# Entries 0 and 1 of the feed-forward block: first product beside the remaining attention, second product by one level of Strassen's scheme

## The chip, the cores and the metric

The kernel runs as one program on one core of a Trainium2 chip. The metric is the device time of an execution in microseconds (us). Before the change it is 1051.8 us, the median of 3 runs (1049.94 to 1052.03).

The core has four engines that compute: TensorE (PE in the rows; its weight loads are PEld), VectorE (DVE), ScalarE (ACT) and GpSimd (POOL). SyncE (SP) issues all transfers here, from one queue in program order. Each engine works through its own list of instructions in order and waits at semaphores. The 16 DMA engines carry the transfers between HBM and on-chip memory.

## The reference

```
attn: (4 entries, 12 heads, 448 rows, 64)
  scores = cap * tanh(q k^T / sqrt(64) / cap);  attn = softmax(scores) v
x = attn, heads side by side              (4, 448, 768)
FFN: xn = layernorm(x) * g
     x  = x + relu(xn w1) w2              w1 (768, 3072), w2 (3072, 768)
gMLP: h = relu(x w_in), w_in (768, 1024); u, v = halves of h
     v = layernorm(v);  v = w_spatial v + b  (over the 448 rows)
     out = (u * v) w_out                  w_out (512, 768)
```

All is float32. Products that need it are made of three TensorE products in a reduced 32-bit format (fp32r): high by high, high by low, low by high part. The inputs that are weights reach the chip as 64-bit floats; ScalarE and VectorE turn each block into float32, and the result is kept in HBM for later use.

## The kernel before

The four entries are worked on in two pairs. **Attention of entries 0 and 1** comes first by itself. Then comes the **FFN of entries 0 and 1, with the attention of entries 2 and 3 beside it**: attention work of the 24 remaining heads is threaded between the matmul units. Then follow the gMLP of entries 0 and 1, the FFN of entries 2 and 3 with nothing beside it, and their gMLP.

The two FFNs are built differently. For entries 0 and 1 the 24 blocks of 128 hidden features are taken in 6 groups of 4: `h_units` makes 4 hidden blocks for both entries (18 matmuls of 448 columns each), which stay on chip in the slots `rb` as high and low part, and `y_units` at once multiplies them into all 6 output blocks (12 matmuls each) and adds the result to the residual in `x`. That is 864 matmuls for the first product and 864 for the second. For entries 2 and 3 both products go by one level of Strassen's scheme, 7 block products in place of 8: `h_four` makes the hidden blocks and writes them, and four mixtures of them, to HBM (`hidden`, 84 tiles of 448 columns), and `y_seven` reads them back product by product. A block product of `y_seven` is 6 steps (`g`) of 18 matmuls, so the second product is 7 x 6 x 18 = 756 matmuls. Its left sides are quarters of `w2` (`a11` to `a22`), or sums and differences of them made by VectorE; a quarter is read out of the kept `w2` in runs of 128 numbers (512 bytes).

The order of instructions on each engine is fixed ahead by a planner (`Program.plan`): it simulates the engines with a cost for each operation and picks, per engine, the ready operation that is due first, provided its buffers have room. Due times follow from the order of TensorE's work. An operation recorded under `prog.either()` may go to one of two engines: the second is taken where the first would keep it waiting longer. Operations under `prog.early()` get a due time of their own. Buffers are slots that go round; some of them belong to a `Stage`, memory that is handed to another set of buffers only when every buffer of the stage before it is free.

The names that matter here: `rs` (16 slots) right-hand sides in two parts, `wh` (3) weights in two parts, `wr` (2) weights as float32, `hs` (10) single tiles of 448 columns, `es` (7) exponentials, `qk` (2) queries and keys, `w` raw 64-bit weights, `kept_...` weights in HBM, `bank` (4) and `two` (2 of two banks) PSUM. In the rows nearly every instruction has line 532, that of the helper that records it, so rows are told apart by names and shapes.

## Time and profile before

| | |
|---|---|
| median of 3 runs | 1051.8 us |
| the profiled execution, whole | 1050.03 us |
| its span, first to last instruction | 1047.9 us |
| TensorE busy in the span | 1030.5 us |
| VectorE, ScalarE busy | 811.2, 501.4 us |
| moved by DMA | 180.25 MB |

The span is 2.1 us shorter than the execution. The stages of the span, by what TensorE does: attention of entries 0 and 1 to about 126.5 us; FFN of entries 0 and 1 with the other attention to 524.1; gMLP to about 633; `h_four` to 786.5; `y_seven` to 941.2; gMLP to the end. Busy times are of one execution; matmuls are pipelined, so that each is shown longer than the time from one to the next, and a busy TensorE is not by itself one at its peak. DMA share is the mean busy share of the 16 DMA engines; it can exceed 1, since packets overlap on an engine.

### The profile page before, as it was taken

Reading aid. Unit: us, or ns where it says so; the run is one execution under the profiler, and the core shown is the slowest. Engines: PE = TensorE matmul, PEld = TensorE weight load, DVE = VectorE, ACT = ScalarE, POOL = GpSimd, SP = SyncE. Lnnn points to the kernel's source line nnn. Section 1 sums busy time; section 2 is a strip of 40 time slices with the busy share of each in tenths; the row PEclk is TensorE's granted clock in tenths of the full one; section 3 lists DMA queues with packets and bytes.
Section 4 is the critical chain, followed back from the end, with each engine's and each line's share of the span. In section 5 each row is a group of like instructions: output and inputs, shape, how many; then the busy total and the mean of one; then the engine's idle time right before and its main releaser. Section 6 shows DMA issues by size and latency. Waiting matters only on the chain.

```text
span 1047.9 us, 14400 instructions
## 1 busy us (share of the span) xinstructions
PE 1030.5 (98%) x5182; PEld 849.7 (81%) x5182; DVE 811.2 (77%) x1395; ACT 501.4 (48%) x780; POOL 14.4 (1%) x19
## 2 busy tenths in 40 slices
PE   7999999999999999999999999999999999999998
PEld 2333698988898879888888889999999899998887
DVE  6979878585686775855979889887787897888971
ACT  7998744355426434453434345544462453324522
POOL 0000000000000000000000110000000000000000
PEclk9999999999999999999999999999999999999999
DMA  7444266467667565554455133455799968302303
GB/s 252 150 132 113 69 192 192 150 205 242 213 214 234 195 225 167 178 183 139 139 175 201 49 111 114 157 183 187 242 335 334 323 183 249 107 29 77 94 31 116
DMA packets 111212, 180.25 MB, mean 172 GB/s; under 512 B 18035, under 2 KB 82213, under 8 KB 111141
## 3 DMA queue, kind: packets, MB, share of 16 engines
q1 hardware_dynamic: 111140, 179.33, 53.9%
q8 instruction: 41, 0.67, 0.3%
q14 instruction: 31, 0.25, 0.1%
HBM read 127.99 MB, written 51.30 MB: 171 GB/s over the span
## 4 chain that ended last, share of the span: by engine, by line
PE 75%; DMA 10%; DVE 10%; ACT 2%; issue 2%; SPq 1%; POOL 0%; ACTq 0%; DVEq 0%; POOLq 0%
PE bank L532 58%; PE two L532 17%; DMA hs<-inv 2%; DVE x L532 2%; DMA inv<-rc 1%; DVE wr L532 1%; DMA qk<-in_qk_dram 1%; DVE wh L532 1%; DMA kept_w<-wr 1%; DMA w<-in_w_dram 1%; DVE es L532 1%; DVE rs L532 1%; DVE small L532 1%; SPq L532 1%; DVE rb L532 1%
## 5 line engine op out<-in xcount | busy, mean ns | idle before, releaser
L532 PE MATMUL bank<-rs,wh 128*128 128x448 f32 x1626 | 342.3, 363 | 3.3 <-DVE rs L532 1.3
L532 PEld LDWEIGHTS bank<-rs,wh 128*128 128x128 f32 x1626 | 304.1, 188 | 28.0 <-DVE wh L532 2.2
L532 PE MATMUL bank<-rb,wh 128*128 128x448 f32 x864 | 175.2, 363 | 0.0
L532 PEld LDWEIGHTS bank<-rb,wh 128*128 128x128 f32 x864 | 161.5, 187 | 12.4 <-DVE es L532 0.6
L532 ACT ACTIVATE wr<-w 128x512 f32<-128x512 f32 (+1 forms) x72 | 53.9, 749 | 112.3 <-DMA w<-in_w_dram 43.9
L532 DVE TENSOR_TENSOR wh<-wr,wh 128x512 fp32r<-128x512 f32 (+2 forms) x116 | 92.6, 801 | 8.9 <-ACT wh L532 6.9
L532 ACT ACTIVATE wh<-wr 128x768 fp32r<-128x768 f32 (+1 forms) x68 | 49.8, 733 | 59.7 <-PE bank L532 43.0
L532 DVE TENSOR_TENSOR x<-bank,x 128x448 f32<-128x448 f32 x95 | 58.7, 621 | 24.2 <-PE bank L532 23.3
L532 ACT ACTIVATE es<-es,capt 128x896 f32<-128x896 f32 x72 | 73.2, 1054 | 0.0
L532 ACT ACTIVATE es<-two,qsc 128x896 f32<-128x896 f32 x62 | 61.7, 1020 | 15.2 <-PE two L532 14.2
L532 PE MATMUL two<-rs,wh 128*128 128x448 f32 x276 | 64.6, 363 | 0.0
L532 DVE SCALAR_TENSOR_TENSOR wr<-w,wr 128x512 int32<-128x512 int32 (+1 forms) x80 | 63.2, 794 | 1.1
L532 PE MATMUL bank<-es,vt 128*64 128x448 f32 x288 | 62.2, 552 | 0.3 <-ACT hs L532 0.3
L532 DVE TENSOR_SCALAR wr<-wr 128x512 int32<-128x512 int32 (+1 forms) x76 | 35.6, 471 | 32.8 <-ACT wr L532 32.6
L532 ACT ACTIVATE hs<-bank 128x448 f32<-128x448 f32 x58 | 31.3, 541 | 53.4 <-PE bank L532 51.1
L532 PEld LDWEIGHTS two<-rs,wh 128*128 128x128 f32 x276 | 51.8, 188 | 3.9 <-DVE wh L532 0.3
L532 ACT ACTIVATE rb<-bank 128x448 fp32r<-128x448 f32 x48 | 26.0, 542 | 58.3 <-PE bank L532 58.0
L532 DVE SCALAR_TENSOR_TENSOR rb<-bank,rb 128x448 fp32r<-128x448 f32 x48 | 29.8, 621 | 30.9 <-ACT rb L532 30.8
L532 DVE TENSOR_TENSOR es<-es,es 128x896 f32<-128x896 f32 x48 | 52.0, 1084 | 0.4 <-ACT es L532 0.2
L532 ACT ACTIVATE rs<-hs 128x448 fp32r<-128x448 f32 x55 | 30.9, 572 | 36.1 <-DMA hs<-h 35.8
L532 DVE TENSOR_TENSOR rs<-hs,rs 128x448 fp32r<-128x448 f32 x75 | 45.5, 620 | 2.4 <-ACT rs L532 2.1
L532 PEld LDWEIGHTS bank<-es,vt 128*64 128x64 f32 x288 | 17.4, 136 | 36.5 <-issue 29.1
(185 smaller groups left out, 1515.6 us busy)
## 6 DMA issues: line engine op xcount, KB each, us to landing
hs<-h SPq DMA_DIRECT2D x84, 224.0 KB
w<-in_w_dram SPq DMA_DIRECT2D x24, 768.0 KB
w<-in_w_dram SPq DMA_DIRECT2D x36, 512.0 KB
qk<-in_qk_dram SPq DMA_DIRECT2D x24, 448.0 KB
h<-hs SPq DMA_DIRECT2D x48, 224.0 KB
kept_w<-wr SPq DMA_DIRECT2D x24, 384.0 KB
kept_w<-wr SPq DMA_DIRECT2D x36, 256.0 KB
wrb<-kept_w SPq DMA_DIRECT2D x24, 384.0 KB
```

The lines of the kernel that those rows point to most:

```text
L532: fn(*(put(a) for a in args), **{k: put(a) for k, a in kw.items()})
```

## The change

The FFN of entries 0 and 1 is cut into two phases. In the first, all 24 hidden blocks of both entries are made (`h_units`, now without groups), with all of the remaining attention beside them, spread over 93% of the phase. The hidden blocks go as single tiles into new slots (`hx`, 10); whenever two blocks of both entries are there, `mixed_h` makes four mixtures and writes all 7 to HBM. The 36 blocks of `w2` are turned into float32 and written to HBM in this phase too. In the second phase `y_seven`, until now used for entries 2 and 3 only, makes the second product. Beside its products 4, 5 and 3 the 16 blocks of `w_in` and `w_out` are turned into float32; before, those of the second half of `w_in` were made inside the gMLP, and the other 10 beside the FFN.

`y_seven` itself changes: the products come in the order 1, 2, 7, 6, 4, 5, 3 (before 1, 7, 6, 4, 5, 2, 3), other sums of blocks are formed, and in the first pass the 24 mixed weight blocks are written to HBM (`kept_s`) and read from there in the second. The stages are new as well: after `one` (attention and first phase) comes `mid` (weights of the second phase), then `gate` (buffers of the gMLP: `rbg`, `vsg`, `qkg`, `bsg`). The planner takes VectorE as second engine of an operation only where the wait for the first is more than 0.8 us longer than the operation itself.

Where the instructions went on TensorE, after the first hidden blocks (`rs` times `wh` into a `bank`, six rows to a block; `rb` are hidden blocks). Before:

```order
L532 MATMUL bank_138<-rs_76,wh_95 128x448 x3
L532 MATMUL bank_138<-rs_77,wh_95 128x448 x3
L532 MATMUL bank_138<-rs_78,wh_95 128x448 x3
L532 MATMUL bank_135<-rb_324,wh_96 128x448 x3
L532 MATMUL bank_135<-rb_325,wh_96 128x448 x3
L532 MATMUL bank_135<-rb_327,wh_96 128x448 x3
L532 MATMUL bank_135<-rb_328,wh_96 128x448 x3
```

And of the changed kernel, at the end of its 24 hidden blocks:

```order
L533 MATMUL bank_137<-rs_76,wh_95 128x448 x3
L533 MATMUL bank_137<-rs_77,wh_95 128x448 x3
L533 MATMUL bank_137<-rs_78,wh_95 128x448 x3
L533 MATMUL bank_140<-rs_63,wh_94 128x448 x3
L533 MATMUL bank_140<-rs_64,wh_94 128x448 x3
L533 MATMUL bank_139<-rs_63,wh_94 128x448 x3
L533 MATMUL bank_139<-rs_64,wh_94 128x448 x3
L533 MATMUL bank_138<-rs_63,wh_94 128x448 x3
L533 MATMUL bank_138<-rs_64,wh_94 128x448 x3
```

The second product followed a group of four hidden blocks out of `rb`; now it starts after the last hidden block, out of `rs`, into three banks at a time.

The transfer queue (SP) in the middle of the first phase, where `h` are hidden tiles and their mixtures on the way to HBM. Before, around the sums of the 6th of 12 pairs of heads of the remaining attention:

```order
L532 DMA kept_w_18_197<-wr_93 128x512
L532 DMA w_331<-in_w_dram 128x1024
L532 DMA kept_w_18_197<-wr_92 128x512
L532 DMA w_330<-in_w_dram 128x1536
L532 DMA vt_0_342<-in_v_dram 128x2x192
L532 DMA qk_339<-in_qk_dram 128x896
L532 DMA qk_340<-in_qk_dram 128x896
L532 DMA sum_10_191<-hs_82 4x448
L532 DMA x_6_186<-hs_84 128x448
```

And of the changed kernel:

```order
L533 DMA kept_w_18_223<-wc_458 128x512
L533 DMA w_460<-in_w_dram 128x1024
L533 DMA h_1_5_224<-hx_456 128x448
L533 DMA hs_83<-inv_6_199 64x448 x2
L533 DMA hs_81<-inv_6_199 64x448 x2
L533 DMA vt_0_463<-in_v_dram 128x2x192
L533 DMA h_2_4_214<-hx_451 128x448
L533 DMA h_6_4_216<-hx_448 128x448
L533 DMA qk_446<-in_qk_dram 128x896
L533 DMA qk_447<-in_qk_dram 128x896
L533 DMA h_7_5_229<-hx_455 128x448
L533 DMA sum_10_221<-hs_80 4x448
```

The writes of hidden tiles stand between the loads of weights and of the attention's inputs.

The transfer queue in `y_seven`: `hs` are hidden tiles read back, `wq` and `wqm` quarters of `w2`. Before (entries 2 and 3, product 6):

```order
L532 DMA wq_6145<-kept_w_18_197 128x6x128
L532 DMA hs_87<-h_6_281 128x448
L532 DMA hs_88<-h_7_288 128x448
L532 DMA wq_6146<-kept_w_24_209 128x6x128
L532 DMA hs_82<-h_8_295 128x448
L532 DMA wq_6147<-kept_w_30_218 128x6x128
L532 DMA hs_81<-h_9_302 128x448
```

And of the changed kernel in the second phase (entries 0 and 1, product 6):

```order
L533 DMA hs_82<-h_6_7_251 128x448
L533 DMA hs_83<-h_6_8_262 128x448
L533 DMA hs_81<-h_6_9_274 128x448
L533 DMA kept_s_0_308<-wqm_3239 128x768
L533 DMA kept_s_0_307<-wqm_3238 128x768
L533 DMA w6m_3250<-in_w_v_dram 128x1024
L533 DMA kept_s_1_310<-wqm_3241 128x768
L533 DMA kept_s_1_309<-wqm_3240 128x768
L533 DMA kept_s_2_312<-wqm_3243 128x768
L533 DMA w6m_3251<-in_w_v_dram 128x1024
L533 DMA hs_85<-h_6_10_285 128x448
```

The same reads of hidden tiles now share the queue with writes of mixed weights and reads of raw `w_in`.

The diff, cut to its core:

```diff
-FIRST = 8, 2, 7, 2
+FIRST = 2, 7, 2, 10, 2, 2
...
-AFTER = 0.3, 0.75, 6
+AFTER = 0.05, 0.9, 0.93
+LATER = 4, 5, 3
...
-                    if alt[k][1] > wait + BIAS:
+                    if alt[k][1] > wait + (BIAS if e != 'V' else -0.8):
...
+    tops = Stage(prog, tc, "sums", (), "right")
     one = Stage(prog, tc, "one")
-    two_h = Stage(prog, tc, "two_h", (one,), "right")
-    two_x = Stage(prog, tc, "two_x", (one,))
...
+    wqm, w6m, wcm = staged(mid, "wq", 18, "wqm"), staged(mid, "w6", 2, "w6m"), staged(mid, "wq", 2, "wcm")
+    rbg, vsg, qkg, bsg = (staged(gate, k, n, k + "g") for k, n in (("rb", 8), ("vt", 7), ("qk", 2), ("acc", 1)))
...
-    wq = staged(four, "wq", 4 * NG)
+    wq = staged(four, "wq", 18)
+    for stage in four, mid:
+        staged(stage, "gap", 1)
+    whf, whm = staged(four, "wh", 3, "whf"), staged(mid, "wh", 1, "whm")
...
-            value(kind, j)
+            value(kind, j, pool=raw6[1])
...
-            raw = w6.get()[:, 0:n]
+            raw = raw6[0 if n > DH else 2].get()[:, 0:n]
-            t = wr.get()[:, 0:n]
+            t = pool.get()[:, 0:n]
...
     def h_unit(b, w):
         hi, lo = w
         ps = banks.get()[:, 0:S]
         mm3(ps, [(hi[:, k], lo[:, k], x[:, 0], x[:, 1]) for k, x in enumerate(xn[b])])
-        t = rb1.get()
-        A.activation(out=t[:, 0, 0:S], in_=ps, func=ACTF.Relu)
-        V.scalar_tensor_tensor(out=t[:, 1, 0:S], in0=ps, scalar=0.0, in1=f(t[:, 0, 0:S]),
-                               op0=ALU.max, op1=ALU.subtract)
-        hq[b % 2].append(t)
-
+        h = hx.get()
+        relu(h, ps)
+        return h
+
+    def relu(o, c):
+        with prog.either():
+            A.activation(out=o, in_=c, func=ACTF.Relu)
+            V.tensor_scalar(out=o, in0=c, scalar1=0.0, scalar2=None, op0=ALU.max)
+
+    def mixed_h(i, h11, h12, h21, h22, t1, t2, t3, t4):
+
+        sub(t1, h12, h11)
+        sub(t2, h22, t1)
+        sub(t3, h22, h12)
+        sub(t4, h21, t2)
+        for n, t in ((1, h11), (3, h22), (2, h21), (5, t1), (6, t2), (7, t3), (4, t4)):
+            hidden[n, i] = dram.tile([128, S], F32, name=f"h{int(last_pass[0])}_{n}_{i}")
+            SP.dma_start(out=hidden[n, i], in_=t)
 
     ysp = []
-
-    def y_unit(b, w, dt, last):
...
-    def y_unit(b, w, dt, last):
-        hi, lo = w
-        ps = banks.get()[:, 0:S]
-        mm3(ps, [(hi[:, i], lo[:, i], h[:, 0, 0:S], h[:, 1, 0:S]) for i, h in enumerate(hq[b % 2])])
-        x = xts[b % 2][dt]
-        V.tensor_tensor(x, ps, x, ALU.add)
-        if last:
-            V.tensor_tensor(x, x, rst[b % 2], ALU.mult)
-            if b % 2 == 0:
-                ysp.append((rs.get(), rs.get()))
-            split_y(b, dt)
...
-            if n == 1:
-                return load(a11, g, wr)
+            if n in (1, 2) or n == 4 and last_pass[0]:
+                held[n, g] = load({1: a11, 2: a12, 4: a22}[n], g, wr if n == 1 else wq)
+                return held[n, g]
+            if last_pass[0]:
+                t = wq.get()[:, 0:HD * FW // 2]
+                SP.dma_start(out=t, in_=kept_s[n, g])
+                return t
             if n == 7:
-                held["a11", g], held["a21", g] = load(a11, g), load(a21, g)
-                t = wr.get()[:, 0:HD * FW // 2]
-                sub(t, held["a11", g], held["a21", g])
+                held["a21", g], t = load(a21, g), load(a11, g)
+                sub(t, t, held["a21", g])
+                keep_s(n, g, t)
+                held["s3", g] = t
                 return t
             if n == 6:
                 held["a22", g] = load(a22, g)
-                s1, s2 = held["a21", g], held["a11", g]
-                add(s1, s1, held["a22", g])
-                sub(s2, s1, s2)
+                s1, s2, x = held["a21", g], held["s3", g], held["a22", g]
+                add(s1, s1, x)
+                sub(s2, x, s2)
+                keep_s(5, g, s1)
+                keep_s(6, g, s2)
                 return s2
+            if n == 5:
+                return held["a21", g]
             if n == 4:
                 return held["a22", g]
-            if n == 5:
-                return held["a21", g]
-            if n == 2:
-                held["a12", g] = load(a12, g)
-                return held["a12", g]
-            s4 = held["a12", g]
-            sub(s4, s4, held["a11", g])
+            s4 = load(a12, g)
+            sub(s4, s4, held["s3", g])
+            keep_s(n, g, s4)
             return s4
+
+        def keep_s(n, g, t):
+            kept_s[n, g] = dram.tile([128, HD * FW // 2], F32, name=f"kept_s{n}_{g}")
+            with prog.early():
+                SP.dma_start(out=kept_s[n, g], in_=t)
 
         X = [banks.get()[:, 0:S] for _ in range(HD)]
         two = twos.get()
         Y = [two[:, 0, 0:S], two[:, 1, 0:S], banks.get()[:, 0:S]]
-        for n, o, start, stop in ((1, X, 1, 0), (7, Y, 1, 0), (6, X, 0, 0), (4, Y, 0, 1), (5, X, 0, 0), (2, None, 1, 1),
-                                  (3, X, 0, 1)):
-            if o is None:
+        beside = deque(beside)
+        two = twos.get()
+        W = [two[:, 0, 0:S], two[:, 1, 0:S]]
+        for n, o, start, stop in ((1, X, 1, 0), (2, W, 1, 1), (7, Y, 1, 0), (6, X, 0, 0), (4, Y, 0, 1), (5, X, 0, 1),
+                                  (3, W, 1, 1)):
+            if n == 2:
+                o = W + [Y[2]]
+            if n == 3:
                 two = twos.get()
                 o = [two[:, 0, 0:S], two[:, 1, 0:S], banks.get()[:, 0:S]]
             for g in range(NG):
+                if beside and n in LATER:
+                    ahead(*beside.popleft())
...
-                w = wh.get()[:, :, 0:HD * FW // 2]
+                w = (wh if n == 1 or g % 2 or g % 4 and not last_pass[0] else whf if last_pass[0] else whm).get()[:, :, 0:HD * FW // 2]
...
-                    t = (r2 if n != 1 and (g + k) % 3 == 0 else rs).get()
+                    t = (r2 if last_pass[0] and n != 1 and (g + k) % 3 == 0 else rs).get()
...
-            b, at, last = {1: (0, 0, 0), 7: (1, HD, 0), 6: (0, HD, 0), 4: (0, HD, 1), 5: (1, HD, 1), 2: (0, 0, 1),
-                           3: (1, 0, 1)}[n]
-            for d in range(HD):
-                y = xts[b][at + d]
-                add(y, o[d], y)
-            if last:
+            for b, at in {1: [(0, 0)], 2: [(0, 0)], 7: [(1, HD)], 6: [(0, HD)], 4: [(0, HD)], 5: [(1, HD), (1, 0)],
+                          3: [(1, 0)]}[n]:
+                for d in range(HD):
+                    y = xts[b][at + d]
+                    add(y, o[d], y)
+            for b, at in {2: [(0, 0)], 4: [(0, HD)], 5: [(1, HD)], 3: [(1, 0)]}.get(n, ()):
                 for d in range(HD):
...
+                    if not last_pass[0]:
+                        V.tensor_tensor(x, x, rst[b], ALU.mult)
...
-    def h_units(bs, g, n):
-
-        steps = [n, FG - n] if n > 2 else [2] * (FG // 2)
-        j0 = g * FG
-        for m in steps:
+    def h_units(bs):
+
+        j0 = 0
+        for m in (4, *[2] * (NF // 2 - 2)):
             w = [weight("w1", j0 + j) for j in range(m)]
-            j0 += m
+            mine = {}
             for b in bs:
                 for j in range(m):
-                    h_unit(b, w[j])
+                    mine[b, j] = h_unit(b, w[j])
                     if b in ln and j == 0:
                         ln_scale(b)
+                    if b % 2 and j % 2:
+                        h = [mine[e, i] for i in (j - 1, j) for e in bs]
+                        mixed_h((j0 + j) // 2, *h, *(hx.get() for _ in range(4)))
                     yield 3 * KD
-
-    def y_units(bs, g, last):
-        if last:
-            for b in bs:
-                xn.pop(b)
-        for dt in range(KD):
-            w = weight("w2", g * KD + dt)
-            for b in bs:
-                y_unit(b, w, dt, last)
-                yield 3 * FG
+            j0 += m
         for b in bs:
-            hq[b % 2].clear()
+            xn.pop(b)
...
-            units = chain(*(x for g in range(NG) for x in (
-                h_units(bs, g, FG if g == 0 and p == 0 else 3 if g == 0 else 2), y_units(bs, g, g == NG - 1))))
-            n = 2 * H if p + 1 < NP else 0
-            total = NG * 2 * (FG * 3 * KD + KD * 3 * FG)
-            todo = []
-            if p == 0:
-                later = [("wv", k) for k in range(KD)] + [("wu", i) for i in range(KH)] + [("wo", k) for k in range(KD)]
-                later = later[AFTER[2]:]
-                for j, x in enumerate(later):
-                    todo.append((total * (AFTER[0] + (AFTER[1] - AFTER[0]) * j / len(later)), ahead, x))
-            drive(units, todo + attend(2 * H * (p + 1), n, 2 * NG * (FG * 3 * KD + KD * 3 * FG) / max(n, 1)))
-            gmlp(bs, [b for b in (2 * p + 2, 2 * p + 3) if n])
+            total = NF * 2 * 3 * KD
+            rows = [("w2", j) for j in range(NG * KD)]
+            later = [("wv", k) for k in range(KD)] + [("wu", i) for i in range(KH)] + [("wo", k) for k in range(KD)]
+            todo = [(total * (AFTER[0] + (AFTER[1] - AFTER[0]) * j / len(rows)), ahead, x) for j, x in enumerate(rows)]
+            n = 2 * H
+            drive(h_units(bs), todo + attend(n, n, AFTER[2] * total / n))
+            raw6[:] = w6m, wcm, w6m
+            y_seven(wqm, later)
+            gmlp(bs, [2 * p + 2, 2 * p + 3])
 
     main()
+    tops.begin()
     one.begin()
     with tc.manual_schedule():
         t = tok_t[0][0]
```

## Rows read from the trace of the kernel before

**Rows 1.** The page: busy time by engine; granted TensorE clock in 40 slices.

```profile
PE 1030.5 (98%) x5182; PEld 849.7 (81%) x5182; DVE 811.2 (77%) x1395; ACT 501.4 (48%) x780; POOL 14.4 (1%) x19
...
PEclk9999999999999999999999999999999999999999
```

**Rows 2.** The page: the chain that ended last, share of the span.

```profile
PE 75%; DMA 10%; DVE 10%; ACT 2%; issue 2%; SPq 1%; POOL 0%; ACTq 0%; DVEq 0%; POOLq 0%
```

**Rows 3.** Busy times by stretch: FFN of entries 0, 1; last `y_seven`.

```profile
core 0: us, PE busy (x) PEld busy (x) DVE busy (x) ACT busy (x) POOL busy (x), PEclk, DMA share, GB/s
126.50:524.10 397.60, 396.45 (x2101) 337.87 (x2099) 283.78 (x464) 177.11 (x261) 1.01 (x1) 1.00 0.59 189
...
786.50:941.20 154.70, 153.73 (x758) 141.48 (x757) 129.16 (x206) 57.54 (x95) 0.00 (x0) 1.00 0.68 206
```

**Rows 4.** Groups of instructions: name and shape, count, busy us, mean ns.

```profile
L532 PE MATMUL bank<-rb,wh 128*128 128x448 f32 x864 | 175.2, 363 | 0.0
```

**Rows 5.** TensorE in order of time at 504 to 530 us: start, length, count.

```profile
503.69 17.17 PE L532 MATMUL bank<-rb,wh 128*128 128x448 f32 x85
520.79 2.48 PE L532 MATMUL bank<-es,vt 128*64 128x448 f32 x12
...
524.08 3.07 PE L532 MATMUL two<-wh,rs 128*128 128x512 f32 x12
...
529.09 1.10 PE L532 MATMUL two<-wh,rs 128*128 128x512 f32 x4
```

**Rows 6.** DMA issues: names, count, KB (1024 bytes) each.

```profile
hs<-h SPq DMA_DIRECT2D x84, 224.0 KB
...
wq<-kept_w SPq DMA_DIRECT2D x24, 384.0 KB
...
w<-in_w_u_dram SPq DMA_DIRECT2D x4, 768.0 KB
w<-in_w_out_dram SPq DMA_DIRECT2D x6, 512.0 KB
w<-in_w_v_dram SPq DMA_DIRECT2D x6, 512.0 KB
...
kept_wu<-wr SPq DMA_DIRECT2D x4, 384.0 KB
kept_wo<-wr SPq DMA_DIRECT2D x6, 256.0 KB
```

**Rows 7.** The same columns as rows 3, where the transfers were busiest.

```profile
785.00:835.00 50.00, 49.62 (x245) 45.24 (x243) 40.31 (x61) 18.72 (x31) 0.00 (x0) 1.00 1.10 337
760.00:780.00 20.00, 20.00 (x102) 18.75 (x101) 17.72 (x30) 14.24 (x26) 0.00 (x0) 1.00 1.02 352
550.00:560.00 10.00, 10.00 (x46) 8.34 (x45) 8.62 (x16) 6.39 (x12) 0.00 (x0) 1.00 1.03 380
```

**Rows 8.** Groups on VectorE, shapes apart.

```profile
L532 DVE SCALAR_TENSOR_TENSOR wr<-w,wr 128x512 int32<-128x512 int32 x48 | 32.8, 687 | 0.7
L532 DVE SCALAR_TENSOR_TENSOR wr<-w,wr 128x768 int32<-128x768 int32 x32 | 30.4, 953 | 0.4
...
L532 DVE TENSOR_SCALAR wr<-wr 128x512 int32<-128x512 int32 x48 | 20.2, 423 | 14.1 <-ACT wr L532 13.9
...
L532 DVE TENSOR_TENSOR wq<-wq,wq 128x768 f32<-128x768 f32 x18 | 17.1, 952 | 0.0
L532 DVE TENSOR_SCALAR wr<-wr 128x768 int32<-128x768 int32 x28 | 15.4, 554 | 18.8 <-ACT wr L532 18.7
...
L532 DVE TENSOR_TENSOR x<-x,rstd 128x448 f32<-128x448 f32 x24 | 14.3, 619 | 0.0
```

**Rows 9.** The same columns as rows 3: gMLP of entries 0, 1.

```profile
560.00:580.00 20.00, 20.00 (x101) 18.75 (x101) 19.76 (x49) 9.80 (x21) 2.34 (x2) 1.00 0.22 77
...
524.10:640.00 115.90, 114.14 (x549) 99.10 (x546) 101.27 (x199) 48.67 (x91) 9.03 (x6) 1.00 0.41 134
```

More of the change, by code (lines that the diff above doesn't have):

```diff
@@ L595, in staged @@
         return stage.slots(name or kind, n, shape, dt, protos[kind])
+    tops = Stage(prog, tc, "sums", (), "right")
     one = Stage(prog, tc, "one")
-    two_h = Stage(prog, tc, "two_h", (one,), "right")
-    two_x = Stage(prog, tc, "two_x", (one,))
+    mid = Stage(prog, tc, "mid", (one,))
+    gate = Stage(prog, tc, "gate", (mid,))
+    two_h = Stage(prog, tc, "two_h", (gate, tops), "right")
+    two_x = Stage(prog, tc, "two_x", (gate,))
     three_h = Stage(prog, tc, "three_h", (two_h,), "right")
@@ L602, in attn_ffn_gmlp_kernel @@
     three = Stage(prog, tc, "three", (four,))
-    rb1, w6, es1, qks = (staged(one, kind, n) for kind, n in zip(("rb", "w6", "es", "qk"), FIRST))
+    w6, es, qks, hx, wc, w4 = (
+        staged(one, kind, n, name) for (kind, name), n in zip(
+            (("w6", "w6"), ("es", "es"), ("qk", "qk"), ("acc", "hx"), ("wq", "wc"), ("w4", "w4")), FIRST))
     vts = [staged(one, "vt", 1, f"vt{i}_") for i in range(2)]
-    accs = [staged(one, "acc", 1, f"acc{i}_") for i in range(2)]
+    wqm, w6m, wcm = staged(mid, "wq", 18, "wqm"), staged(mid, "w6", 2, "w6m"), staged(mid, "wq", 2, "wcm")
+    rbg, vsg, qkg, bsg = (staged(gate, k, n, k + "g") for k, n in (("rb", 8), ("vt", 7), ("qk", 2), ("acc", 1)))
+    accs = [staged(tops, "acc", 1, f"acc{i}_") for i in range(2)]
     h2 = staged(two_h, "acc", 6, "hh")
@@ L963, in ln_load, with feature_sum @@
             SP.dma_start(out=xts[b % 2][k], in_=xsp[b, k])
-    def feature_sum(ps, x, pool=rb1):
+    def feature_sum(ps, x, pool=wh):
         t = pool.get()[:, :, 0:S]
@@ L977, in ln_mean @@
         ps = banks.get()[:, 0:S]
-        feature_sum(ps, accof[b])
+        feature_sum(ps, accof[b], rs if b >= 2 else wh)
         means[b] = rst[b % 2] if b >= 2 else hs.get()
@@ L1063, in v_mm @@
         os = [t[:, j] for t in two for j in range(2)] + [banks.get() for _ in range(len(cs) - 4)]
-        single = (0, 1, KD // 2, KD // 2 + 1, KD // 2 + 2, KD - 1) if last_pass[0] else (0, KD - 1)
-        order = [*range(KD // 2, KD), *range(KD // 2)] if last_pass[0] else [*range(KD)]
+        single = 0, 1, KD // 2, KD // 2 + 1, KD // 2 + 2, KD - 1
+        order = [*range(KD // 2, KD), *range(KD // 2)]
         for at, k in enumerate(order):
@@ L1078, in v_mm @@
                     part.close()
-        if last_pass[0]:
-            vs = [vs3.get() for _ in os]
-        else:
-            vs = [es.get().rearrange("p a n -> p (a n)")[:, 0:DH] for _ in os]
+        vs = [(vs3 if last_pass[0] else vsg).get() for _ in os]
         for vi, o in zip(vs, os):
@@ L1140, in sp_units @@
                                  stop=(b % 2 == 1 and c == half - 1 and m == 2))
-        xs = None if last_pass[0] else qks.get()
+        xs = None if last_pass[0] else qkg.get()
         for b, ps in zip(bs, pss):
@@ L1193, in gmlp @@
             scale(b)
-        bias = xts[0][KD - 1] if last_pass[0] else vts[0].get()[:, 0:S]
+        bias = xts[0][KD - 1] if last_pass[0] else bsg.get()
         SP.dma_start(out=bias, in_=b_sp)
@@ L1404, in snap @@
             A.activation(out=o, in_=ps, func=ACTF.Copy)
-        def relu(o, c):
-            with prog.either():
-                A.activation(out=o, in_=c, func=ACTF.Relu)
-                V.tensor_scalar(out=o, in0=c, scalar1=0.0, scalar2=None, op0=ALU.max)
         product(1, X, True, False)
@@ L1427, in h_four, with y_seven @@
         relu(h21, X)
-        sub(t1, h12, h11)
-        sub(t2, h22, t1)
-        sub(t3, h22, h12)
-        sub(t4, h21, t2)
-        for n, t in ((1, h11), (3, h22), (2, h21), (5, t1), (6, t2), (7, t3), (4, t4)):
-            hidden[n, i] = dram.tile([128, S], F32, name=f"h_{n}_{i}")
-            SP.dma_start(out=hidden[n, i], in_=t)
+        mixed_h(i, h11, h12, h21, h22, t1, t2, t3, t4)
     hidden = {}
     def second_pass(bs):
+        hidden.clear()
         for i in range(NF // 2):
             h_four(i)
-        y_seven()
-    def y_seven():
+        y_seven(wq)
+    def y_seven(wq, beside=()):
         HD = KD // 2
```

11 lines of the change are left out of this document (3 added, 8 removed).

## The prediction

> **What bounds the kernel now.** I read the page's busy times first, then the chain of waits, then the busy times by stretch. TensorE is busy for 1030.5 of 1047.9 us, at the full granted clock in every slice [rows 1], and the chain that ended last is TensorE for 75% of the span [rows 2]; so nearly every matmul that goes is worth its time, and nearly every other operation that goes is worth nothing while it stays hidden. The reader is to see next how full the stretches are that the change touches [rows 3]. In the FFN of entries 0 and 1 TensorE is idle for 397.6 - 396.45 = 1.15 us; VectorE is busy for 71%, ScalarE for 45%, the DMA engines for 59%. In the last `y_seven`, the code that the change uses a second time, TensorE is idle for 0.97 us, but VectorE is busy for 129.2 of 154.7 us, and the DMA engines for 68%. The change shortens the first stretch by TensorE work alone, and keeps nearly all of its transfers.
>
> **Removed: the second product in groups.** 864 matmuls read `rb` [rows 4]. 85 of them in a row take 520.79 - 503.69 = 17.10 us [rows 5], 0.2012 us each; 864 x 0.2012 = 173.8 us. (Their group's busy time of 175.2 us agrees with it.) The first phase, with everything else on TensorE left as it is, is then 397.6 - 173.8 = 223.8 us.
>
> **Added: the second product by `y_seven`.** 756 matmuls, as in the last `y_seven`, which takes 154.7 us with its own waits [rows 3], against 756 x 0.2012 = 152.1 without any. I take 154.7. The exchange is worth 173.8 - 154.7 = 19.1 us.
>
> **VectorE in the first phase.** The split of each hidden block into a low part goes (48 instructions), and 48 subtractions for the mixtures come, on the same 448 columns: nothing. What goes with the second product (72 additions to `x`, 36 splits of weights, ten conversions) relieves it by far more than nothing. So the 283.8 us of [rows 3] fall to about 190 to 200 in 223.8; VectorE does not bound there. ScalarE keeps about its 177 us, 79% of the shorter phase. A pair of heads of the attention comes every 0.93 x 223.8 / 12 = 17.3 us in place of 33, so a late exponential has half the cover; the price of that is open, and I take 0: 79% leaves room.
>
> **VectorE in the second phase.** To the 129.2 us of the last `y_seven` come the conversions, each a shift and a combination: 12 x (0.423 + 0.687) + 4 x (0.554 + 0.953) = 19.3 us, and 12 multiplications by `rstd` of 0.619, 7.4 us [rows 8]; 155.9 us for 154.7 of TensorE. VectorE is full. The gMLP already has such a stretch: VectorE busy 19.76 of 20 us, and TensorE 20.00 [rows 9]. So a full VectorE can be free; the bounds are 0 and, if every product waits a little for its last split, about 8 us. I take 2, since the planner puts more of the copies on ScalarE, which has only 57.5 us there.
>
> **Mixed weights kept.** In the last `y_seven` 24 sums of 0.952 us go [rows 8], 22.8 us of VectorE, and 24 reads in runs of 512 bytes become plain ones. All that lies behind TensorE, which idles 0.97 us there. I take 0.5 us off, at most 1.
>
> **gMLP of entries 0 and 1.** Six conversions leave it; TensorE idles 115.9 - 114.1 = 1.8 us there in all [rows 9], so between 0 and 1.8 us can come back. I take 0.
>
> **The transfers, the term that decides.** The FFN moved 189 GB/s over 397.6 us, 75.1 MB [rows 3]. Ten conversions leave the first phase: 4 x (768 + 384) + 6 x (512 + 256) KB = 9.4 MB [rows 6]. The hidden tiles come, as many as in the last pass (84 x 224 KB [rows 6]): 19.3 MB. That makes 85.0 MB in 223.8 us, 380 GB/s. The second phase reads 84 hidden tiles (19.3 MB), 36 quarters of weights (36 x 384 KB, 14.2 MB), writes 24 mixed ones (9.4 MB), reads 16 raw blocks (9.4 MB) and writes them (4.7 MB): 57.0 MB. They must have landed before the buffers of the gMLP open (stage `gate`), which TensorE needs when the gMLP's first product is done: six blocks of 21 matmuls, 529.09 - 524.08 = 5.01 us each [rows 5], 30.1 us. So 142.0 MB have 223.8 + 154.7 + 30.1 = 408.6 us, a mean of 348 GB/s for longer than the trace shows anything like it. Bounds [rows 7]: for 10 us 380 GB/s were moved, by which all is done in 374 us and costs nothing; for 50 us 337, in the mix of hidden tiles and 512-byte runs that the second phase has; for 20 us 352, in the mix of tile writes and weights that the first has. By the nearest rows 85.0 / 0.352 + 57.0 / 0.337 = 411 us, 2 more than there are. The other end is the FFN's own bytes per busy time, 189 / 0.59 = 320 GB/s at a share of 1: 444 us, 35 over. Between 0 and 35 I take 7: the 2, and 5 for gaps, since SyncE issues in order and a write that waits for VectorE holds back the loads behind it. In the busiest 50 us TensorE lost 0.38 us [rows 7], so short shortages are covered by the 10 `hs` and 16 `rs` slots; long ones are not.
>
> The Trainium skill ("DMA: Bandwidth & Descriptors", Specifications) gives about 358 GB/s as what HBM grants one core; by that figure alone 142.0 MB would need 397 us, and the change would lose nothing to transfers. The trace has both more, 380, and, in the mix of the second phase, less, 337 [rows 7]; the measured rates decide.
>
> The same table puts the smallest transfer at full rate at 512 bytes, which is just the run in which the quarters of `w2` are read. By it those reads would cost no more than others; the stretch that holds them has 337 / 1.10 = 306 GB/s to a share of 1, against 380 / 1.03 = 369 in the other [rows 7], so the trace speaks against counting on it.
>
> **The sum.** The profiled execution took 1050.0 us, 2.1 more than its span and 1.8 less than the median. 1050.0 - 19.1 - 0.5 + 2 + 7 = 1039.4; against the median that is 1041.2. I forecast 1041 us, 10.6 faster.
>
> **Rivals.** *Transfers set the pace.* If the queue sustains less than 142.0 / (408.6 + 18) = 333 GB/s from the first hidden tile to the gMLP, the wait outweighs the 18 us left of the gain, and the kernel is slower than before. At 320 GB/s it is 1051.8 - 17.6 + 35 = 1069. For it: the FFN's bytes per busy time, and that no stretch over 50 us shows a share over 1.10. Against it: the two stretches at 352 and 380 GB/s had shares of only 1.02 and 1.03, so that they may not have been full, and writes of converted `w_out` and mixed weights can lag. TensorE would stand still in the second phase and ahead of the gMLP's second product, where the new buffers open.
>
> *VectorE binds the second phase.* The 155.9 us count in full and each product's last split comes late: 8 in place of 2, with transfers as taken: 1047. For it: 101% of demand. Against it: the same engine at 99% without harm [rows 9].
>
> *Nothing waits.* The transfers run as in the 10 us at 380, the second product takes 152.1 us, and the gMLP loses its 1.8: 1051.8 - 173.8 + 152.1 - 1 - 1.8, which is 1027. For it: tile slots that cover 18 us of reads (10 `hs`, two to a step of 18 matmuls, 3.6 us). Against it: the last `y_seven` had 2.6 us of waits with 25 MB less.
>
> *The change does not do what it says* in one part: the kept mixed weights save VectorE time that nothing waited for, and add 9.4 MB of writes to the fullest stretch. That is in the sums above, at 0.5 us against 28 us of transfer time.
>
> **How the numbers follow.** Chances: forecast (1033 to 1047) 0.43; nothing waits 0.12; VectorE binds 0.08; transfers set the pace 0.37, of which 0.08 end within 0.2% of the time before, 2.1 us, which is about what a measurement of this kernel can tell from no change, and 0.29 above. Faster is 0.43 + 0.12 + 0.08 = 0.63, same 0.08, slower 0.29. The range runs from 1028, a microsecond above the case without waits, to 1069, the transfers at 320 GB/s; the forecast's own is 1033 to 1047.
>
> **What would show it.** Right: the stretch from the first hidden blocks to the last lasts 224 to 232 us, `y_seven` for entries 0 and 1 155 to 163, with DMA shares of 1.0 or more in both and VectorE at 95% or more in the second; the last `y_seven` as long as before, with VectorE some 20 us less busy. Wrong in the term of the transfers: TensorE idle for more than 15 us in these phases, released by loads (`hs` from `h`, raw `w`, `wqm`) or by whatever they release. Wrong in the first term: the attention beside the first phase, at half the distance, makes TensorE wait for ScalarE's exponentials with the DMA share well under 1.

## The result, and the profile after

The changed kernel takes 1036.9 us (median of 4 runs, 1033.3 to 1039.3) against 1051.4 (4 runs, 1049.9 to 1052.0) for the kernel before: a ratio of 0.9861, 95% interval 0.983 to 0.9892. The forecast was 1041. The profiled execution is the fastest of the four, 1033.3 us with a span of 1031.5, so its stages are to be read against the 1050.0 us of the profiled execution before.

The page's busy times, the granted clock in 40 slices and the chain that ended last, in the kernel after; they answer to [rows 1, 2].

```profile
PE 1009.9 (98%) x5074; PEld 828.6 (80%) x5074; DVE 828.4 (80%) x1405; ACT 573.9 (56%) x903; POOL 17.3 (2%) x21
...
PEclk9999999999999999999999999999999999999999
...
PE 72%; DMA 14%; DVE 8%; ACT 3%; issue 2%; SPq 1%; POOL 1%; DVEq 0%; ACTq 0%; POOLq 0%
```

TensorE is busy for 20.6 us less with 108 matmuls fewer, and the span is 16.4 us shorter: 4 us went into waits. The stretches of the kernel after follow, with the columns of [rows 3] (stretch, its length, busy time and instructions by engine, granted clock, DMA share, GB/s): the first phase, the second product of entries 0 and 1, both with the 30 us behind them that the prediction had counted in, the gMLP of entries 0 and 1, and the last `y_seven`.

```profile
127.30:350.30 223.00, 223.00 (x1236) 175.60 (x1235) 180.69 (x290) 162.28 (x239) 2.20 (x2) 1.00 0.99 351
350.30:512.30 162.00, 155.78 (x764) 142.04 (x763) 138.83 (x216) 80.54 (x130) 0.00 (x0) 1.00 1.04 353
127.30:542.30 415.00, 408.78 (x2127) 341.79 (x2126) 342.42 (x546) 256.12 (x392) 2.20 (x2) 1.00 0.98 340
512.30:620.30 108.00, 106.13 (x510) 92.32 (x509) 93.50 (x178) 51.17 (x97) 12.03 (x8) 1.00 0.41 130
774.40:925.60 151.20, 151.20 (x758) 141.72 (x757) 114.76 (x200) 47.84 (x76) 0.00 (x0) 1.00 0.72 239
```

Stage by stage, before to after: lead +0.8; FFN 397.6 to 223.0 + 162.0, -12.6; gMLP 109.4 to 108.0, -1.4; next first product 153.0 to 154.1, +1.1; last `y_seven` 154.7 to 151.2, -3.5; last gMLP -0.8. The sum is -16.4, which is the difference of the spans. The first phase has no TensorE wait at all, beside DMA engines that are full for 223 us. All the waits of the FFN lie in the second product. Here is TensorE in order of time where it waits (start, length, matmuls, in brackets the wait ahead of them and what ended it):

```profile
369.95 0.68 PE L533 MATMUL bank<-rs,wh 128*128 128x448 f32 x2 [1.43 <-ACT wh L533]
...
398.63 1.67 PE L533 MATMUL two<-rs,whm 128*128 128x448 f32 x7 [1.76 <-DVE whm L533]
...
495.28 1.87 PE L533 MATMUL two<-rs,wh 128*128 128x448 f32 x8 [0.46 <-DVE rs L533]
...
499.93 0.47 PE L533 MATMUL two<-rs,wh 128*128 128x448 f32 x1 [0.69 <-DVE rs L533]
...
597.87 3.90 PE L533 MATMUL bank<-rs,wh 128*128 128x448 f32 x18 [1.47 <-DVE qkg L533]
```

And the stretches in which they fall, with one between them for comparison:

```profile
360.00:380.00 20.00, 18.09 (x88) 15.94 (x87) 12.83 (x20) 9.47 (x14) 0.00 (x0) 1.00 1.11 311
380.00:400.00 20.00, 18.24 (x92) 16.76 (x91) 14.28 (x21) 8.54 (x13) 0.00 (x0) 1.00 1.15 321
420.00:440.00 20.00, 19.60 (x98) 18.03 (x98) 19.49 (x31) 12.15 (x20) 0.00 (x0) 1.00 1.05 403
480.00:500.00 20.00, 18.64 (x90) 16.06 (x88) 19.74 (x33) 9.29 (x15) 0.00 (x0) 1.00 1.02 373
```

At 360 to 400 the DMA share is highest and the rate lowest, and VectorE has time to spare: the waits look like the transfers'. At 480 to 500 VectorE is busy for 19.74 of 20 us: those look like VectorE's. The experiments ask whether that is so.

### The profile page after: what moved, and what is told of

Read it like the earlier page. It is cut to its first block, busy times and chain, and to the rows that moved or that the text cites. A ratio compares the mean times of both kernels' runs of the same rounds, so it can differ in the third digit from the quotient of the medians.

```text
span 1031.5 us, 14887 instructions
## 1 busy us (share of the span) xinstructions
PE 1009.9 (98%) x5074; PEld 828.6 (80%) x5074; DVE 828.4 (80%) x1405; ACT 573.9 (56%) x903; POOL 17.3 (2%) x21
## 4 chain that ended last, share of the span: by engine, by line
PE 72%; DMA 14%; DVE 8%; ACT 3%; issue 2%; SPq 1%; POOL 1%; DVEq 0%; ACTq 0%; POOLq 0%
PE bank L533 51%; PE two L533 20%; DMA hs<-h 3%; DMA wqm<-kept_w 3%; DMA hs<-inv 1%; DVE x L533 1%; DVE wh L533 1%; SPq L533 1%; DMA h<-hs 1%; DMA wrb<-kept_w 1%; DMA inv<-rc 1%; DVE hs L533 1%; DMA qk<-in_qk_dram 1%; ACT rs L533 1%; DVE rs L533 1%
## 5 line engine op out<-in xcount | busy, mean ns | idle before, releaser
L533 PE MATMUL bank<-rs,wh 128*128 128x448 f32 x1806 | 378.8, 363 | 3.7 <-DVE qkg L533 1.5
L533 PEld LDWEIGHTS bank<-rs,wh 128*128 128x128 f32 x1806 | 337.1, 187 | 33.4 <-issue 2.8
L533 DVE TENSOR_TENSOR rs<-hs,rs 128x448 fp32r<-128x448 f32 x159 | 95.1, 621 | 6.3 <-ACT rs L533 5.9
L533 DVE TENSOR_TENSOR wh<-wr,wh 128x768 fp32r<-128x768 f32 (+2 forms) x80 | 67.9, 855 | 27.1 <-ACT wh L533 26.9
L533 ACT ACTIVATE rs<-hs 128x448 fp32r<-128x448 f32 x123 | 68.4, 572 | 37.5 <-DMA hs<-h 36.7
L533 ACT ACTIVATE wh<-wr 128x768 fp32r<-128x768 f32 (+2 forms) x70 | 53.3, 763 | 38.4 <-PE bank L533 16.5
L533 PE MATMUL two<-qk 64*128 64x448 f32 x168 | 41.8, 603 | 4.7 <-DMA qk<-in_qk_dram 4.2
L533 PE MATMUL two<-wh,rs 128*128 128x512 f32 x144 | 35.8, 395 | 0.0
L533 PE MATMUL bank<-rx,whb 128*128 128x448 f32 x144 | 32.7, 362 | 0.0
L533 PE MATMUL two<-rx,whb 128*128 128x448 f32 x144 | 32.7, 362 | 0.0
```

Of the source, the lines that this page charges most:

```text
L533: fn(*(put(a) for a in args), **{k: put(a) for k, a in kw.items()})
```

## Experiments

All times are medians of 4 to 12 runs; each ratio is to the kernel before on the same chip. Differences of two ratios whose intervals overlap are called not told apart.

### Waits of the second product: transfers or VectorE

The changed kernel again, as the base of this group:

> The changed kernel again, beside the others on one chip. 1034 to 1039 us, 0.983 to 0.989 of the time before. Of its 1031.5 us of span one execution showed 223.0 us for the first phase without an idle microsecond of TensorE in it, and 160.6 us for the second, 9.4 over 756 matmuls at 0.2 us. Theory T: these 9.4 come from the transfers at the second phase's start, where reads in runs of 512 bytes bring the DMA share to 1.11 to 1.15 at only 311 to 321 GB/s. Rival V: they come from VectorE, which is nearly full there.

Measured: 1036.4 us, ratio 0.9842 (0.9823 to 0.9862).

Longer runs for the quarters of `w2`, by another order of its columns in HBM (the line that reorders them is not shown):

```
...
-            in_=kept2[g][:, q[0]].rearrange(... "p (d a n) -> p d a n", a=2, n=128)[:, :, q[1]])
+            in_=kept2[g][:, q[0]].rearrange("p d (a n) -> p d a n", a=2)[:, :, q[1]])
```

> The same bytes, but the columns of w2 lie so that a quarter is read in runs of 1024 bytes in place of 512. By T the share at the start of the second phase falls from 1.11 to 1.15 towards 1.03, its rate rises from 316 to some 350 to 370 GB/s, and TensorE waits 3 to 6 us less: 1031 to 1034 us. By V nothing changes: 1036 to 1038.

Measured: 1033.3 us, 0.9819 (0.9798 to 0.9841). The same stretches as above, in this kernel:

```profile
360.00:380.00 20.00, 18.41 (x83) 16.42 (x82) 13.81 (x21) 10.95 (x17) 0.00 (x0) 0.91 1.06 329
380.00:400.00 20.00, 20.00 (x102) 18.75 (x101) 16.48 (x24) 8.47 (x14) 0.00 (x0) 1.00 1.09 366
```

The wait near 399 is gone, at 366 GB/s in place of 321 for a smaller share of the DMA engines; the one near 369 stays. VectorE shows how the wait hung on the reads. In the profile of the changed kernel above it does this at that time:

```profile
396.75 0.96 DVE L533 TENSOR_TENSOR wqm<-wqm,wqm 128x768 f32<-128x768 f32 x1 [1.36 <-DMA wqm<-kept_w]
397.62 0.95 DVE L533 TENSOR_TENSOR whm<-wqm,whm 128x768 fp32r<-128x768 f32 x1
```

It waits 1.36 us for a quarter that a sum needs, and only behind that sum makes the low part `whm` that TensorE waits for. With the longer runs the low part is made 3.6 us earlier, 0.6 of which the kernel was ahead in any case:

```profile
394.00 0.96 DVE L533 TENSOR_TENSOR whm<-wqm,whm 128x768 fp32r<-128x768 f32 x1 [0.43 <-ACT whm L533]
```

The traces also have the time of each packet: between 380 and 400 us a packet of 512 bytes took 32 ns on average in the base, one of 1024 bytes 50 ns here. Then without the 24 sums that mix the weights in the first `y_seven` (left out: these sums alone, the transfers are the same):

```
-                sub(t, t, held["a21", g])
...
-                add(s1, s1, x)
-                sub(s2, x, s2)
...
-            sub(s4, s4, held["s3", g])
```

> The 24 sums and differences of weight blocks are left out in the second phase (the blocks are used and kept unmixed), so that VectorE has 22.9 us less to do there, with all transfers as they are. By V the 9.4 us of waits nearly go: 1028 to 1030 us. By T only the waits late in the phase go, which end at VectorE's splits, some 2 us: 1034 to 1036.

Measured: 1035.9 us, 0.9829 (0.9807 to 0.9851), not told apart from the base. Its waits of 1.36 and 0.46 us at 492 and 497 remain, so the waits near 497 are not the sums'; what makes them is open. The wait near 399 is absent here too, but this does not clear the reads: the low part is made at 397.62 as in the profile above, and TensorE comes to it only at 398.66, 2.3 us later, mostly since it lost more near 371 (a wait of 1.95 us, then 16 matmuls in 5.01 us for 3.48 in the base). So the runs of 512 bytes are shown as a cause near 399, together with the sum that stands behind them. By the medians they cost 3.1 us here, and 4.9 in a second pair of kernels below (1035.9 and 1031.0); in either pair the two intervals overlap a little.

### Had the first phase's transfers room?

```
+            if not last_pass[0]:
+                SP.dma_start(out=dram.tile([128, S], F32, name=f"again_{n}_{i}"), in_=t)
```

> The changed kernel with every mixed hidden tile of the first phase written to HBM twice (84 more writes of 229 KB, 19.3 MB, into tiles that nothing reads). It asks whether the transfers of the first phase have room. There 75 MB move in 213 us at a DMA share of 0.99 with no TensorE wait. If a share near 1.0 means a full queue (the prediction's rival on transfers), 19.3 MB at 351 GB/s are 55 us more, and the time is 1075 to 1095. If the queue is only well filled because loads are issued as early as their buffers allow, the extra bytes go at a higher rate (up to the 400 GB/s that the second phase shows at a share of 1.04) and the phase grows by 0 to 10 us: 1037 to 1048.

Measured: 1103.0 us, 1.0494 (1.0469 to 1.0519), 66 us more than the base. From the first hidden block to the end of the waits, and a stretch within:

```profile
127.00:437.00 310.00, 261.80 (x1334) 200.65 (x1333) 208.71 (x328) 177.96 (x257) 3.10 (x2) 0.93 0.99 348
...
380.00:400.00 20.00, 6.81 (x19) 4.64 (x18) 7.41 (x12) 4.07 (x6) 0.00 (x0) 0.59 0.97 335
```

TensorE stands idle for 48 us and the rate does not rise: in this mix about 350 GB/s at a share of 0.99 is all there is. The changed kernel's first phase, 351 GB/s, is therefore full and has no room for more. The matmuls were slower as well: 1334 take 261.8 us at a mean granted clock of 0.93, where the base takes some 243 (an estimate: 223.0 for its first 1236, and 0.2 for each further one). Whether that is where the 11 us over the 55 that the bytes need come from is not shown.

### What the kept mixed weights are worth

They are not kept; both passes mix (the buffers stay as changed):

```
-            if n in (1, 2) or n == 4 and last_pass[0]:
+            if n in (1, 2):
-            if last_pass[0]:
-                t = wq.get()[:, 0:HD * FW // 2]
-                SP.dma_start(out=t, in_=kept_s[n, g])
-                return t
...
-            with prog.early():
-                SP.dma_start(out=kept_s[n, g], in_=t)
+            pass
```

> The mixed weights are not kept: 9.4 MB of writes leave the second phase, 9.4 MB of reads in the last y_seven change back to 512-byte runs, and its 24 sums come back. By T the writes fall behind the stretch in which TensorE waits, so the second phase gains 0 to 3 us; the last y_seven, 151.2 us in the changed kernel and 154.7 before, loses its 3.5 again: 1037 to 1041 us. If instead the writes themselves are what TensorE waits for, the second phase falls to 153 and the kernel to about 1033. By V as by T: the sums of the first pass stay.

Measured: 1045.8 us, 0.9936 (0.9916 to 0.9955). And with the weights kept, but the split weights in the old buffers `wh` alone, without `whf` and `whm`:

```
-                w = (wh if n == 1 or g % 2 or g % 4 and not last_pass[0] else whf if last_pass[0] else whm).get()...
+                w = wh.get()...
```

> The changed kernel with the split weights of both Strassen products in the two old buffers alone (the three extra ones of the last product and the one of the first are not used). It asks how much of the last product's 151.2 us (154.7 before) comes from these buffers rather than from mixed weights that are read back. If the weights read back carry it, the last product stays at 151 to 152 us and the time within 1 us of 1036.4. If the buffers carry it, the last product takes 153 to 155 us and the time is 1038 to 1041.

Measured: 1048.2 us, 0.9968 (0.9954 to 0.9983). The last `y_seven` in three kernels, each in a fence of its own: the base, not kept, old buffers alone.

```profile
776.00:928.30 152.30, 152.30 (x763) 142.76 (x762) 115.98 (x201) 48.82 (x78) 0.00 (x0) 1.00 0.74 241
```

```profile
777.70:934.70 157.00, 154.15 (x764) 143.98 (x763) 131.10 (x210) 57.15 (x93) 0.00 (x0) 0.99 0.73 219
```

```profile
773.30:940.10 166.80, 158.90 (x763) 144.43 (x763) 116.26 (x202) 47.29 (x77) 0.00 (x0) 0.98 0.68 220
```

The old buffers `wh` are three, not two as the expectation has it, and the changed kernel adds three to them in this product (`whf`). Without the kept weights the kernel takes 9.4 us more, where the prediction had 0.5; without the added buffers 11.9 us more, past both sides of what was expected. Neither half works alone in the changed kernel; neither run is the kernel before with one half added, since the order of the products is the changed one in both.

The stretches hold a few matmuls of the neighbours. Counted over the 756 of the product alone, the last `y_seven` takes 151.2 us in the base, 155.8 with the weights not kept and 165.6 with the old buffers alone. So it accounts for 4.6 of the 6.5 us by which the profiled execution without kept weights is longer than the base's. The second product of entries 0 and 1, from which the 9.4 MB of writes are gone, got 1.9 us longer (161.6 to 163.5) in place of 0 to 3 shorter: the writes are not what TensorE waited for there.

Without the kept weights VectorE is 15 us busier in the last `y_seven`, and one wait of 2.85 us appears. With the old buffers alone VectorE is as free as in the base, but the hand-over of a buffer shows. ScalarE, then TensorE, in that kernel:

```profile
829.83 0.84 ACT L533 ACTIVATE wh<-wq 128x768 fp32r<-128x768 f32 x1 [5.62 <-PE bank L533]
...
830.73 0.67 PE L533 MATMUL two<-rh,wh 128*128 128x448 f32 x2 [0.73 <-ACT wh L533]
...
832.19 0.47 PE L533 MATMUL two<-rh,wh 128*128 128x448 f32 x1 [0.79 <-DVE wh L533]
```

ScalarE's copy had waited 5.62 us for TensorE to let the buffer go, and TensorE then waits 0.73 us for the copy and 0.79 for the low part that VectorE makes from it. Six such hand-overs make 8 us of waits; TensorE's busy time is 6.6 us longer for the same 763 matmuls, at a mean clock of 0.98. In the base such a copy starts well ahead: one at 827.57 is for matmuls from 831.17 on. Why the kernel before did not stumble on the same three buffers ([rows 3]: 0.97 us idle) stays open.

### The wait in the gMLP of entries 0 and 1

In the base this wait is longer than in the profile above: 1.09 us at 595 and 2.75 at 601, and the 18 matmuls behind it take 5.46 us in place of 3.90. TensorE in the base, and then its VectorE at that time:

```profile
595.06 0.67 PE L533 MATMUL bank<-rs,wh 128*128 128x448 f32 x2 [1.09 <-DVE rs L533]
...
600.89 5.46 PE L533 MATMUL bank<-rs,wh 128*128 128x448 f32 x18 [2.75 <-DVE qkg L533]
```

```profile
590.52 3.95 DVE L533 SCALAR_TENSOR_TENSOR x<-x,g_t,rstd 128x448 f32<-128x448 f32 x5
594.39 0.61 DVE L533 TENSOR_TENSOR rs<-qkg,rs 128x448 fp32r<-128x448 f32 x1
...
596.45 3.86 DVE L533 SCALAR_TENSOR_TENSOR x<-x,g_t,rstd 128x448 f32<-128x448 f32 x6 [0.90 <-DMA rstd<-rstd]
600.23 1.14 DVE L533 TENSOR_TENSOR qkg<-bank,accg 128x448 f32<-128x448 f32 x2
```

My first theory was GpSimd, to which the changed planner gives 4 gate multiplications instead of 2. Without that choice, on the changed kernel and on the one with longer runs:

```
-                for e in (V, P):
+                for e in (V,):
```

> The changed kernel with the gate multiplication offered to VectorE alone, nothing else altered. By the theory on the gated block: 1031 to 1034 where the changed kernel has 1036.4 (waits of 1.09 and 2.75 us at 594 to 601 gone, the 18 matmuls behind them at 3.9 us instead of 5.46). By the rival: 1035 to 1038.

> The kernel with runs of 1024 bytes for the last weight (1033.3 measured) and the gate multiplication of the gated blocks offered to VectorE alone, not to GpSimd. Theory on the gated block: the two waits of TensorE near 592 and 595 (1.06 and 2.75 us) come from gate products that GpSimd is given (2.35 us each), and the low rate of the 18 matmuls behind them (5.48 us where 3.90 are usual) goes with the wait; without them the time is 1028 to 1031. Rival: the gate products only queue on VectorE instead, which is busy there as well, and a wait of the same size stays: 1032 to 1035.

Measured: 1035.9 us, 0.9848 (0.9824 to 0.9871), and 1031.0 us, 0.9807 (0.9784 to 0.983); neither is told apart from its base. One wait of 3.38 and 3.10 us stands where two had stood, now released by the split `rs`. GpSimd alone is not the cause. The rows above name another: the 12 products that normalise entries 2 and 3, 0.67 us each, which stand on VectorE ahead of the last gated tiles, with a wait for the row `rstd` in their middle (0.90 us). Three kernels were to place them later:

```
-            if i == 3:
+            if i == 5:
```

> The kernel with 1024-byte runs and the gate multiplication on VectorE alone (1031.0 measured), and with the 12 products that normalise the next two entries placed behind the gated block's last unit instead of its fourth. In the run before it TensorE waited 3.10 us for the split of a gated tile, which VectorE did behind 11 of these products (588.46 to 592.1, with 1.43 us of waiting for the deviation's row among them). Theory: the order on VectorE makes the wait, so it goes, the gated block takes 3 us less, and the time is 1027 to 1029. Rival: the products are only late then, and the next block's splits wait for them by as much: 1030 to 1033.

> As the kernel above, but with GpSimd allowed for the gate multiplication as in the changed kernel (the planner then gives it 2 of the 12, as before the change, instead of 4). If the 12 products are what pushed the two extra multiplications to GpSimd, the waits near 592 and 595 (1.06 and 2.75 us, with 1.6 us of slow matmuls behind them) go here as well and the time is 1028 to 1030. If GpSimd's 2.35 us by itself is what TensorE waits for, one wait of 1 to 3 us stays: 1030 to 1033.

The third of them also ended the conversions of `w2` earlier (`AFTER = 0.05, 0.8, 0.93`):

> The kernel of the first of these three, and the conversions of the second weight spread over the first 80% of the first phase instead of 90%. Theory on the hand-over: the wait at 367 to 371 (0.8 to 2.6 us in four runs) is for quarters of that weight whose conversions end last, so it goes: 0.5 to 2 us less than the first of these three. Rival: it is for the last hidden tiles, which are computed last in any case, and the queue of the first phase (share 0.99) is full, so earlier conversions make waits there: 0 to 5 us more.

The block has only four units, so a place behind the sixth never comes: these three kernels leave the 12 products out, and their times are read as that. Measured: 1025.0 us, 0.975 (0.9726 to 0.9773); 1027.3, 0.977 (0.9748 to 0.9793), with 2 multiplications on GpSimd; 1026.0, 0.9772 (0.9744 to 0.98). There is no TensorE wait left in the gated block in any of them, GpSimd or not. Ending the conversions earlier changed nothing that can be told, and its wait at 371 is 1.13 us against 1.92, within what that wait varies by; a new wait of 1.65 us, for ScalarE, stands at 207 in the first phase. At last with all 12 products, placed by need:

```
-                with prog.early():
-                    for b in nxt:
-                        normalise(b)
+                for b in nxt:
+                    normalise(b)
```

> The kernel with 1024-byte runs and the gate multiplication on VectorE (1031.0 measured), in which all 12 products that normalise the next two entries are computed, but are placed by when the next product needs them and no longer as early as possible. In the three runs before this one these 12 products were left out, which took 4 to 6 us. On VectorE the splits of the gated tiles stand ahead of all but a few of them here. If their place on VectorE was the price, the wait of 3.1 us before the last gated tiles goes and the time is 1025 to 1029, the 12 products hidden behind the output product's matmuls. If their work was the price (7.3 us of VectorE wherever it stands), the wait moves to the start of the next first product and the time is 1030 to 1033.

Measured: 1032.8 us, 0.9787 (0.9759 to 0.9814); the runs were 1026.7 and 1028.2 at a mean clock of 1.000 and 1032.8, 1033.0 and 1033.4 at 0.997 or 0.998. TensorE in the profiled one, a run of the second kind:

```profile
372.37 5.68 PE L533 MATMUL bank<-rs,wh 128*128 128x448 f32 x18 [3.57 <-ACT wh L533]
...
626.93 0.67 PE L533 MATMUL bank<-rs,whb 128*128 128x448 f32 x2 [0.59 <-DVE rs L533]
...
631.84 1.11 PE L533 MATMUL bank<-rs,wab 128*128 128x448 f32 x3 [1.24 <-ACT rx L533]
```

The wait of 3.1 us in the gated block is gone, and 1.8 us of it are back at the start of the next first product, as the rival had it. So the 12 products, with the wait for `rstd` among them, are shown to be the cause, and moving them is worth little: the wait moves along and is 1.3 us shorter. This kernel, with longer runs and the gate on VectorE, has the lowest ratio of those that compute everything, not told apart from 0.9807 but below the base's.

## Why the prediction was right, point by point

**The exchange of products** was right in both halves. First phase: 223.8 forecast, 223.0 measured. Second product: 154.7 + 2 + 7 = 163.7 forecast, 162.0 measured, of which 6.2 us are idle and the rest 756 matmuls and the first few of the gMLP. The first phase came out a microsecond under the 224 to 232 that were named as a sign, since TensorE waits nowhere in it.

**VectorE in the first phase**, at 181 us against the 190 to 200 forecast, and **ScalarE**, at 162 against 177, make TensorE wait nowhere: the attention at half the distance cost nothing, as taken.

**The transfers** were right in mechanism and nearly in size. 351 and 353 GB/s over the two phases are what [rows 7] said for such mixes (352 and 337), and the bytes to 542 us, 340 x 415 = 141 MB, are the 142.0 counted. Their place was not as counted: of the 85.0 MB put into the first phase 78.3 moved in it (351 x 223), and the rest later, without a wait of TensorE in the first phase. The waits that they release or that fall in their fullest stretch (1.43, 1.76 and some of 0.3 to 0.4 us) are about 4 us for the 7 taken. The 35 us end of the range rested on bytes by busy time, 320 GB/s at a share of 1; the run gives 351 / 0.99 = 355. But the rival was real: 84 writes more cost 66 us, so there was no room, and the kernel stands just on the right side of it. The Trainium skill ("Perfetto Trace Analysis", Roofline) allows a core that works alone more than 358 GB/s, up to about 435 by its DMA engines. The trace agrees in one mix, 403 here, and not in the other, where the full queue gave 348.

**VectorE in the second phase** was to be at 95% or more: it is at 139 of 162 us, 86%, 17 less than the 155.9 counted. Two things make that up. VectorE does 10 copies there, against 32 in the last `y_seven` of the kernel before, which is 9.4 us; the others went to ScalarE, which has 81 us. And 3 of the 16 conversions and 9 of the 12 multiplications by `rstd` come only after this stretch, about 9 us. At its end, 480 to 510, the waits are 1.7 us for the 2 taken.

**The kept mixed weights** are the step that was mis-sized: -0.5 forecast, "All that lies behind TensorE, which idles 0.97 us there". The last `y_seven` is 3.5 us shorter, the 0.97 us of idle time and 2.5 of small losses that made 758 matmuls take 153.7 us before and 151.2 after; idle time was no bound on what could be had. VectorE is 14.4 us less busy, not 20. The reads were miscounted too: there were 30 of quarters before, and there are 18 and 24 of kept blocks now, so that this product reads more, about 36 MB (239 x 151.2) for 32 (206 x 154.7). The prediction did not price the three added buffers at all. The 3.5 us belong to the kept weights and the buffers together: taken out of the changed kernel one at a time, they cost 4.6 and 14.4 us in this product, and 9.4 and 11.9 by the medians of the whole. How much of it is the order that the planner then chooses is not shown.

**The gMLP** was taken as 0 and gave 1.4 us in this execution; in the base's it took 2.7 (111.7 us for the 510 matmuls that took 109.0 before). The kernel before has a wait of 1.29 us in this place; here it is 1.47, and in the base 1.09 and 2.75. The prediction read VectorE's load there [rows 9] and not what stands in its queue.

The forecast of the profiled execution was 1039.4; it took 1033.3. Of the 6.1 us, 3.0 are the last `y_seven`, 1.7 the second product, 1.4 the gMLP and 0.8 the first phase, -1.1 the other stages and 0.3 outside the span. Part of this is luck of one execution, the fastest of four: the others took 1036.6 to 1039.3, and in the base's, at 1036.2, the gMLP is 3.5 us longer.

## What to carry to other kernels

When a product leaves a stage whose transfers stay, divide the bytes of the shortened stage by its new length and look for the same mix elsewhere in the trace at a DMA share near 1: that rate, not bytes by busy time, is the limit. Idle time of TensorE is no upper bound on what a stage can gain: here 758 matmuls without waits came closer together by 2.5 us. An edit that takes work away and adds buffers has two prices, and taking them out one at a time showed 4.6 and 14.4 us where the two together had given 3.5. When an engine in order is late with a small split, list what stands ahead of it on that engine before suspecting a slower engine that shares the work.

## What the runs showed of the hardware

Short waits of TensorE can cost more than their length, and the length does not decide it. In the base the 18 matmuls behind a wait of 2.75 us took 5.46 us, and 5.68 behind 3.57 us in the last kernel above, where 18 take 3.90 at the full granted clock; the slice of 20 us then shows a mean of 0.91, that is, part of it at 1.2 GHz in place of 2.4. In the kernel without kept weights the same matmuls behind the same wait show no loss:

```profile
603.48 3.87 PE L533 MATMUL bank<-rs,wh 128*128 128x448 f32 x18 [2.75 <-DVE qkg L533]
```

Behind the wait near 370, 16 matmuls took 3.48 us after 2.24 us of it in the base, and 5.05 after 1.27 us in the kernel with longer runs. What decides it is open. The executions differ by it in part: the changed kernel and most of its variants have a mean clock of 0.993 to 0.998, the kernel before mostly 0.998 to 1.000, and the two fastest runs of the last kernel, at 1.000, are 4.6 to 6.7 us shorter than the other three. Why the wait at the hand-over of the two phases varies from 0.8 to 3.6 us is open.

At a DMA share of about 1 the rate differed with the mix: 348 to 351 GB/s with tile writes and weight reads, 304 to 322 at the start of the second product with reads in runs of 512 bytes, 329 and 366 with runs of 1024 in the same place, 403 to 412 further on. The packets go with it: on average those of 512 bytes took 32 ns between 380 and 400 us, those of 1024 bytes 50 and those of 1792 bytes about 80, which is 16, 20 and 22 bytes per ns; those of 3072 bytes took 121 ns between 420 and 440 us, 25 bytes per ns. Without the sums, runs of 512 bytes went with 356 GB/s between 380 and 400 us, with a third fewer such packets in that stretch; so the rate tells of the mix in a stretch and not of the runs alone.
